# Loading the first K tile in four strided parts in a decode attention kernel

## Chip, cores, metric

One core of a Trainium2 chip. The metric is the device time of one execution in microseconds; lower is better. Executions of one kernel agree within 0.1% here (1271.40 to 1271.73 us for the kernel before), and all runs told below were in the fast state. Every set of runs was timed in rounds beside the kernel before on the same chip. In the names below PE is the tensor engine, DVE the vector engine, ACT the scalar engine, and SP the sync engine, which issues the large loads here.

## The reference, cut

A gated sum of one attention block at decode (one new token, a cache of 32,768 positions) and one small dense block.

```python
B, Sq, D = 2, 1, 448
Hq, Hkv, Sk, Dh = 16, 8, 32768, 256          # k_cache, v_cache: (B, Hkv, Sk, Dh), bf16
q = x @ wq                                   # (2, 16 heads, 256)
p = softmax(q k^T * Dh**-0.5);  a = (p v) @ wo
b = gelu(x @ w1 + b1) @ w2 + b2
out = g * a + (1 - g) * b                    # g = sigmoid((x * gate_w).sum(-1))
```

Each of the two caches is 268 MB; with the weights, the work is reading 547 MB once. Everything else is small.

## The kernel before: the parts that matter

K and V come in tiles of 16,384 positions. A tile has 128 partitions; partition p holds 128 consecutive positions of 256 values, that is one contiguous row of 65,536 bytes. Three slots of a ring in SBUF take the tiles in turn; SP issues all large loads.

```python
P, R = 128, 128
SLOT = R * Dh                                 # 32768 bf16 = 65,536 bytes per partition
ring = sb("ring", [P, NB * SLOT], dt.bfloat16)            # NB = 3

def kv_src(cache, idx):
    ...
    return cache[b, kvh, t*P*R:(t+1)*P*R, :].rearrange("(p r) d -> p (r d)", p=P)

def first_load(E):                            # placed ahead of the opening barrier
    s0 = slot_of[("K", 0)]
    E.ins(lambda e: e.dma_start(cut(s0, 0, SLOT), kv_src(A_k_cache, 0)),
          key=("fill", ("K", 0)), stream=f"slot{s0}")

def prog_sp(E):                               # then WQ, W1, K1, K2, V0, K3, V1, ...
    for d in order[1:]:
        for pd in before_of[d]:
            E.wait("pe", released(pd))        # until the slot is free
        ...
        dma(lambda e, ...: e.dma_start(cut(slot_of[d], 0, SLOT), src), f"slot{slot_of[d]}", ("fill", d))

def T(idx, blk):                              # DVE: first user of a K tile
    if blk == 0:
        wait_fill(E, ("K", idx))
    E.ins(lambda e: e.transpose(k_words(idx, blk), k_words(idx, blk)), key=("T", idx, blk))
```

The load queue (q1 in the profile) is one deep line, and its packets follow the order of issue: in the kernel before the first packet of WQ, 24,576 bytes long, starts at 21.01 us by the packet records, when all 128 rows of the first tile have started. SP puts the next tile in long before the last one has landed: K1 is issued at 2.78 us, and the last row of K0 ends at 21.8 us.

## Time and profile before

| | before |
|---|---|
| median (6 runs) | 1271.53 us |
| span of the profiled run | 1269.6 us |
| share of 16 DMA engines that the load queue fills | 99.8% |
| first K tile used | 22.17 us |
| time for one row of 65,536 bytes on one engine | 2.42 us |

The lines, and how they are read, are in the prediction.

### The profile page before, as it was taken

The numbers are of one execution on the slowest core, as the hardware profiler recorded it, in microseconds if no ns is written. First come the engines' busy times: TensorE is split into PE (matmuls) and PEld (weight loads), VectorE is DVE, ScalarE is ACT, GpSimd is POOL, SyncE is SP. The second block draws the span as 40 slices with busy tenths as digits, with TensorE's granted clock in tenths as the row PEclk, the third lists the DMA queues.
The fourth block names the chain that finished last, engine by engine and source line by source line (L and its number), as shares of the span: only waits on it lengthen the run. The fifth ranks groups of instructions, "written<-read, shape, count | busy, mean of one in ns | idle before, by whom it ended". The sixth has DMA issues, their size and how long they took to land.

```text
span 1269.6 us, 7458 instructions
## 1 busy us (share of the span) xinstructions
PE 699.4 (55%) x4386; PEld 141.0 (11%) x1842; DVE 690.0 (54%) x311; ACT 44.7 (4%) x184; POOL 4.4 (0%) x19
## 2 busy tenths in 40 slices
PE   0977457635466554665544665444664546655365
PEld 0211001100011110111000111000110001111012
DVE  4676536655365563556735467453755636557351
ACT  0100000000000000000000000000000000000000
POOL 1000000000000000000000000000000000000000
PEclk9888787776788677877767877778877678877787
DMA  9999999999999999999999999999999999999998
GB/s 407 451 429 428 432 432 432 447 432 428 429 432 434 438 432 440 434 432 429 432 429 442 432 436 438 432 429 429 432 442 432 434 440 432 429 429 432 442 424 371
DMA packets 11114, 547.58 MB, mean 431 GB/s; under 512 B 1368, under 2 KB 1632, under 8 KB 2144
## 3 DMA queue, kind: packets, MB, share of 16 engines
q1 hardware_dynamic: 10948, 547.43, 99.8%
q8 instruction: 7, 0.11, 0.0%
q10 hardware_dynamic: 156, 0.01, 0.0%
q14 instruction: 3, 0.02, 0.0%
HBM read 547.43 MB, written 0.00 MB: 431 GB/s over the span
## 4 chain that ended last, share of the span: by engine, by line
DMA 61%; PE 19%; DVE 14%; issue 5%; SPq 0%; ACT 0%; ACTq 0%
DMA ring<-in_A_k_cache_dram 57%; DVE ring L758 12%; PE ps_s L525 6%; PE ps_s L342 6%; PE ps_o L342 4%; DMA ring<-in_A_wo_dram 3%; DVE mx L762 1%; DMA PT<-in_gate_w_dram 1%; PE ps_o L574 1%; PE ps_m L539 0%; PE ps_m L534 0%; DVE gmax L764 0%; PE ps_o L468 0%; DVE gmx L768 0%; PE ps_o L439 0%
## 5 line engine op out<-in xcount | busy, mean ns | idle before, releaser
L758 DVE STREAM_TRANSPOSE ring<-ring 128x4096 uint32<-128x4096 uint32 x128 | 557.6, 4413 | 379.8 <-DMA ring<-in_A_k_cache_dram 379.6
L525 PE MATMUL ps_s<-ring,Abd 128*128 128x512 bf16 x1024 | 424.9, 415 | 399.9 <-DVE ring L758 399.4
L342 PE MATMUL ps_s<-ring,Abd 128*128 128x512 bf16 x1024 | 421.2, 411 | 0.0
L525 PEld LDWEIGHTS ps_s<-ring,Abd 128*128 128x128 bf16 x1024 | 105.7, 103 | 819.3 <-DVE ring L758 462.0
L342 PE MATMUL ps_o<-ring,PT 128*24 128x512 bf16 x1504 | 114.0, 411 | 0.0
L544 PE MATMUL ps_f<-o_sb,selg 128*32 128x257 f32 x32 | 17.0, 634 | 91.1 <-DVE o_sb L791 89.9
L574 PE MATMUL ps_o<-ring,PT 128*24 128x512 bf16 x544 | 57.9, 424 | 12.8 <-DMA ring<-in_A_v_cache_dram 12.8
L762 DVE TENSOR_REDUCE mx<-ps_s 128x1 f32<-128x1024 f32 x16 | 19.6, 1225 | 62.8 <-PE ps_s L342 62.8
L675 ACT ACTIVATE negm<-ps_m 128x1 f32<-128x1 f32 x16 | 2.7, 171 | 1131.8 <-PE ps_m L539 1131.8
L775 DVE STREAM_TRANSPOSE PT<-pexp 128x1024 bf16<-128x1024 bf16 x16 | 19.9, 1244 | 39.7 <-PE ps_o L342 39.7
L791 DVE TENSOR_REDUCE o_sb<-ps_o 128x256 f32<-128x2048 f32 x15 | 34.4, 2291 | 0.5
L789 DVE TENSOR_TENSOR ps_o<-ps_o,mask 128x2048 f32<-128x2048 f32 x15 | 34.3, 2290 | 0.0
L574 PEld LDWEIGHTS ps_o<-ring,PT 128*24 128x24 bf16 x544 | 14.7, 99 | 104.8 <-issue 87.9
L772 DVE COPY ls<-lsum 128x1 f32<-128x1 f32 x16 | 2.5, 154 | 32.1 <-ACT pexp L679 32.1
L669 ACT COPY Abd<-qrep 32x16 bf16 (+1 forms) x128 | 19.5, 199 | 0.6
L679 ACT ACTIVATE pexp<-ps_s,negm 128x1024 bf16<-128x1024 f32 x16 | 17.8, 1114 | 1.7
L534 PE MATMUL ps_m<-ident_f,mx 128*1 128x128 f32 x32 | 6.1, 271 | 21.1 <-DVE mx L762 21.1
L439 PE MATMUL ps_o<-ring,xT 128*32 128x512 bf16 x16 | 6.2, 608 | 20.5 <-issue 20.5
L544 PEld LDWEIGHTS ps_f<-o_sb,selg 128*32 128x32 f32 x32 | 2.9, 140 | 109.5 <-DVE o_sb L791 107.4
L539 PE MATMUL ps_m<-ones_f,gmx 1*128 1x1 f32 x32 | 6.4, 267 | 9.9 <-DVE gmx L768 9.9
L805 DVE TENSOR_SCALAR o_sb<-ps_o,mask 128x256 f32<-128x256 f32 x1 | 0.5, 484 | 15.6 <-PE ps_o L342 15.6
L764 DVE TENSOR_REDUCE gmax<-ps_m 1x2 f32<-1x128 f32 x16 | 4.4, 278 | 7.5 <-PE ps_m L534 7.5
(87 smaller groups left out, 78.0 us busy)
## 6 DMA issues: line engine op xcount, KB each, us to landing
ring<-in_A_v_cache_dram SPq DMA_DIRECT2D x1, 4096.0 KB, 27.2
ring<-in_A_v_cache_dram SPq DMA_DIRECT2D x2, 2048.0 KB, 34.0
ring<-in_A_wq_dram SPq DMA_DIRECT2D x1, 3072.0 KB, 28.6
ring<-in_B_w_dram SPq DMA_DIRECT2D x1, 1568.0 KB, 32.9
ring<-in_A_wo_dram SPq DMA_DIRECT2D x1, 1568.0 KB, 36.2
ring<-in_B_w_dram SPq DMA_DIRECT2D x1, 1344.0 KB, 32.2
ring<-in_A_wo_dram SPq DMA_DIRECT2D x1, 1008.0 KB, 38.2
ring<-in_A_wo_dram SPq DMA_DIRECT2D x1, 560.0 KB, 39.1
```

The source lines that it names most:

```text
L342: return e.add_instruction(mybir.InstMatmult(name=f"I-{nc.next_id()}", engine=mybir.EngineType.PE, ldweights=False, ins=[e.lower_ap(x), e. ...
L525: fn = lambda e, o=o, x=x, st=st, sp=sp, s=s, w=w: e.matmul(o, a_win(s, w), x, start=st, stop=sp, skip_group_check=True)
L539: E.ins(lambda e: e.matmul(ps_m[:, C_BC:C_BC + 1], gmx[:, :], ones_f[0:1, 0:1], start=True, stop=True), key=("M2", g))
L544: E.ins(lambda e: e.matmul(ps_oa, selg[:, :], o_sb[:, :], start=False, stop=False, skip_group_check=True), key=("OT", g))
L574: fn = lambda e, o=o, x=x, wt=wt, st=st, sp=sp, j=j: e.matmul(o, wt, x, start=st, stop=sp, skip_group_check=True)
L669: E.ins(lambda e, o=o, Q=Q, c=c: e.copy(o[:, :, c:c + 2], qrep[32 * Q:32 * Q + 32, :, bass.ds(E.dyn(2 * g, 2), 2)]), key=(("A", g) if (Q = ...
L679: E.ins(lambda e: e.activation(pexp[:, :].rearrange("p (r i a) -> p i r a", r=CR, i=2), ps_s[:, :].rearrange("p (i r a) -> p i r a", i=2, ...
L758: E.ins(lambda e: e.transpose(k_words(idx, blk), k_words(idx, blk)), key=("T", idx, blk))
L762: E.ins(lambda e: e.tensor_reduce(mx[:, :], ps_s[:, :], AX.X, ALU.max), key=("MX", g))
L775: E.ins(lambda e: e.transpose(PT[:, :], pexp[:, :]), key=("PT", g))
L789: E.ins(lambda e: e.tensor_tensor(p, p, mb, ALU.mult), key=("OM", g))
L791: E.ins(lambda e: e.tensor_reduce(o_sb[:, 0:Dh], ps_o[:, :].rearrange("p (n d) -> p d n", d=Dh), AX.X, ALU.add), key=("OS", g))
```

## The change

The intent, as far as the code tells it: let the first transfer be small, one row for each engine, then one more, two and four, so that the stream might start sooner. The partitions are taken in steps of 8, 8, 4 and 2: (0, 8, ..., 120), (4, 12, ..., 124), (2, 6, ..., 126), and all the odd ones.

```diff
         def first_load(E):
             s0 = slot_of[("K", 0)]
-            E.ins(lambda e: e.dma_start(cut(s0, 0, SLOT), kv_src(A_k_cache, 0)), key=("fill", ("K", 0)), stream=f"slot{s0}")
+            src = kv_src(A_k_cache, 0)
+            for i, (r, step) in enumerate(((0, 8), (4, 8), (2, 4), (1, 2))):
+                o = ring[r:P:step, s0 * SLOT:(s0 + 1) * SLOT]
+                E.ins(lambda e, o=o, r=r, step=step: e.dma_start(o, src[r:P:step, :]),
+                      key=(("fill", ("K", 0)) if i == 3 else f"fill{i}"), stream=f"slot{s0}")
```

## The prediction

The sum that was named had these terms: eight rows, each 2.42 us longer, +19.4 us; less 1 us that engines out of step were to give back; together +18.4 us and 1289.9 us; less a few tenths for an earlier start, 1289.5 us. That a row would take 2 x 2.42 us: take it, and what sets the rivals A, B and C apart, as assumption.

> **What bounds the kernel now**
>
> I read four views in this order: the page's rows by slice and by queue, the chain of work, the stretches of one microsecond at the start, and the order of time of the SP queue with what it waits for.
>
> The page first.
>
> ```profile
> span 1269.6 us, 7458 instructions
> ...
> DMA  9999999999999999999999999999999999999998
> GB/s 407 451 429 428 432 432 432 447 432 428 429 432 434 438 432 440 434 432 429 432 429 442 432 436 438 432 429 429 432 442 432 434 440 432 429 429 432 442 424 371
> ...
> q1 hardware_dynamic: 10948, 547.43, 99.8%
> ...
> DMA 61%; PE 19%; DVE 14%; issue 5%; SPq 0%; ACT 0%; ACTq 0%
> ```
>
> The queue of SP moves 547.43 MB and its packets fill 99.8% of what 16 engines have in the span. No slice falls below 9 tenths until the last one. PE (55%) and DVE (54%) are far from full. So the time is: the moment at which data begins to flow, plus 547.43 MB at the rate of the engines, plus the tail. Nothing that shortens compute can matter, and every microsecond that the DMA engines lose, wherever it is lost, comes out at the end, because there is no idle DMA time later in which to catch up.
>
> Then the first microseconds. Columns are PE, PEld, DVE, ACT, POOL busy, the clock, the DMA share and GB/s. A packet counts wholly in the stretch in which it starts.
>
> ```profile
> 0.00:1.00 1.00, 0.00 (x0) 0.00 (x0) 0.00 (x0) 0.00 (x0) 0.40 (x6) 1.00 0.00 0
> 1.00:2.00 1.00, 0.00 (x0) 0.00 (x0) 0.69 (x1) 0.00 (x0) 0.96 (x7) 1.00 3.17 1049
> 2.00:3.00 1.00, 0.00 (x0) 0.00 (x0) 1.00 (x1) 0.00 (x0) 1.00 (x3) 1.00 0.00 0
> 3.00:4.00 1.00, 0.00 (x0) 0.00 (x0) 1.00 (x8) 0.00 (x0) 1.00 (x5) 1.00 0.00 0
> 4.00:5.00 1.00, 0.00 (x0) 0.00 (x0) 0.26 (x1) 0.00 (x0) 0.85 (x4) 1.00 2.42 1049
> ```
>
> 1049 GB/s for 1 us is 1.049 MB, or 16 packets of 65,536 bytes: one row of K per engine (128 rows of 256 bf16). A share of 3.17 says that each of these first sixteen took 3.17 us; the second sixteen took 2.42 us each. So one row costs an engine 2.42 us (27.1 GB/s, times 16 is 433 GB/s, the rate of the whole run), and the first row about 0.75 us more, a start-up cost. All engines begin together and go in step: sixteen starts in one stretch, none in the next two, sixteen again.
>
> Last, the SP queue and the first use of the tile.
>
> ```profile
> 0.00 0.40 SPq L374 DMA_DIRECT2D ring<-in_A_k_cache_dram  x1
> 0.81 0.80 SPq L388 DMA_DIRECT2D ring<-in_A_wq_dram  x2
> 1.66 1.07 SPq L393 DMA_DIRECT2D ring<-in_B_w_dram  x2
> ...
> 22.17 17.42 DVE L758 STREAM_TRANSPOSE ring<-ring 128x4096 uint32<-128x4096 uint32 x4 [0.62 <-DMA ring<-in_A_k_cache_dram]
> ...
> SPq L100 <- PE ps_o L473: 42.5, 1, 42.5
> ...
> SPq L864 <- PEq L864: 0.8, 1, 0.8
> ```
>
> The first K tile is issued ahead of the opening barrier, in 0.40 us; the first packets start just after 1.0 us; the tile has landed by about 22.1 us. That is 1.05 + 3.17 + 7 x 2.42 = 21.2 us for the eight rows of an engine, and under 1 us to the semaphore and for late engines. SP then waits for PE at the barrier. The next load that waits for a buffer is issued at about 45.8 us.
>
> [...]
>
> **The change part by part**
>
> Removed: one issue of 0.40 us. Added: four. By the rows above an issue costs about 0.40 us (0.80 for two), so SP reaches the barrier at about 4 x 0.42 = 1.7 us in place of 0.4, and the barrier, which ended near 0.8 us, ends near 1.8 us. That delays the set-up on all engines by about 1 us. It costs nothing: the first tile is in the queue by then, DVE waits for it until 22 us, and the weights queue behind it.
>
> Start of the data: [...] The sixteen first packets all start between 1 and 2 us, so under 0.5 us can be gained.
>
> The bytes: the same 128 rows from the same addresses, the same 65,536-byte packets. If I divide each transfer in order, engine e gets row 8e, then 8e+4, then 8e+2 and 8e+6, then 8e+1, 8e+3, 8e+5 and 8e+7. [...]
>
> A row then takes an engine 2 x 2.42 = 4.84 us. For the tile: 8 x 2.42 = 19.4 us more. [...] Net +18.4 us. After the first tile everything is 128 partitions again and costs what it did. Because the DMA engines have no slack, the 18.4 us stand in the end: 1271.5 + 18.4 = 1289.9, and less a few tenths for the earlier start, 1289.5 us.
>
> The waits beside it: [...] the gate's weights, which landed at 19.25 us, would land near 38 us. The query weights, which follow the first tile, move from about 30.8 to about 50 us, so they still come later. The next load's wait (45.8 us) moves to about 65, while the queue then holds data until 54 + 19 = 73 us (8.4 MB, 3.7 MB, 1.6 MB and 8.4 MB at 433 GB/s end near 54 us now). So no second gap opens.
>
> **The rivals**
>
> A, no effect. The engines could be chosen by the partition itself[...]: the first two transfers then go to different engines and run at once, and all rows are moved as before. For it: the even 2.42 us of today. [...] Time 1271 to 1272 us; at best 0.5 us is gained from the start.
>
> B, half the effect. [...] Then only two rows cost double: 2 x 2.42 = +4.8 us, 1276 us. Or [...] anywhere from 1276 to 1288. [...]
>
> C, the main line: all eight rows at half rate, 1288 to 1291 us.
>
> D, worse than C: [...] the larger distance of 512 KB between the rows read at once (eight rows of 65,536 bytes) slows the reading as well. It would take 25.4 us to pass 2%, a factor of 2.3 on the tile. I see no line for it.
>
> **Range and chances**
>
> I give C 0.52, B 0.2, A 0.22, D 0.06. The time that I name is C's, 1289.5 us. The range from 1271.0 to 1292.5 covers A's lower edge up to a C without any relief (1271.5 + 19.4 = 1290.9), and nearly 9 in 10. It is wide because the distribution has two humps. Faster by 2% would need 25 us less than a stream that is already 99.8% full; that is excluded in practice, 0.005. Slower by over 2% is D, 0.055. Within 2%: 0.94.
>
> **What will show it right or wrong**
>
> In the stretches of 1 us: a second wave of packets that starts near 6.5 us, in place of 4-5 us, and shares near 4.8 in the first 40 us, show C. Double shares for two waves only show B; 3.17 and then 2.42 show A. The first transpose on DVE at about 41 us is C, 27 is B, 22 is A. The first two slices of the page's GB/s row should fall well below 400, the rest stay as they are. SP's first issue should be four, ended near 1.7 us, and the weights' issue begin near 1.9 us. The query's first matmul moves from 30.8 to about 50 us in C. I am wrong if [...] rows are not dealt out in order.

## The result, and the profile after

| | before | after |
|---|---|---|
| median (6 runs each) | 1271.53 us | 1276.65 us |
| lowest to highest | 1271.40 to 1271.73 | 1276.52 to 1277.01 |
| span of the profiled run | 1269.6 us | 1274.8 us |

The ratio is 1.0041 (95% interval 1.0028 to 1.0054). Ratios here are the mean time of one kernel's runs over that of the other's of the same rounds, so not quite the ratio of the medians. It is a loss of 5.1 us, well outside the noise and well within 2%. The direction and the verdict were as predicted; the size was not: 18.0 us were named.

The page of the changed kernel:

```profile
span 1274.8 us, 7471 instructions
...
GB/s 344 446 428 428 431 440 439 426 430 439 430 440 432 428 432 438 430 444 428 428 434 436 434 440 428 428 438 434 436 436 428 430 440 430 442 430 428 432 430 372
...
q1 hardware_dynamic: 10996, 547.43, 99.8%
```

The bytes are the same and the queue is still 99.8% "busy", though 5 us longer: a packet that takes twice as long counts as busy all that time (in the stretch from 5 to 10 us a share of 0.98 at 210 GB/s, where the kernel before has 0.97 at 420). Only the first slice fell, from 407 to 344 GB/s. A slice is 31.9 us, so 63 GB/s less are 2.0 MB, and 2.0 MB at 433 GB/s are 4.6 us. Nearly the whole loss lies in the first 32 us.

The stretches of 1 us at the start of the changed kernel (columns as in the prediction; the last two are DMA share and GB/s, each packet counted where it starts):

```profile
1.00:2.00 1.00, 0.00 (x0) 0.00 (x0) 0.00 (x0) 0.00 (x0) 0.00 (x0) 1.00 4.54 983
2.00:3.00 1.00, 0.00 (x0) 0.00 (x0) 0.00 (x0) 0.00 (x0) 0.00 (x0) 1.00 0.29 66
...
5.00:6.00 1.00, 0.00 (x0) 0.00 (x0) 1.00 (x8) 0.00 (x0) 1.00 (x3) 1.00 0.92 197
6.00:7.00 1.00, 0.00 (x0) 0.00 (x0) 0.20 (x2) 0.00 (x0) 0.91 (x4) 1.00 3.99 852
```

Fifteen packets start in the first stretch and one in the second. The share is that of 16 engines, so these sixteen take 4.54 + 0.29 = 4.83 us each on the mean. The next sixteen (3 + 13) take 0.92 + 3.99 = 4.9 us. In the kernel before these two numbers were 3.17 and 2.42. Sixteen rows that start together like this, one for each engine, are called a wave from here on. A transfer of 16 rows keeps all 16 engines busy (share 0.97 and 0.98 in the two stretches of 210 GB/s below), at half their speed: sixteen rows are in flight at a time, as before, and the queue holds 48 packets more (10,996 for 10,948), which are packets of 4 bytes, 16 for each of the three transfers more.

Then it stops. Stretches of 5 us, the first two of the kernel before and then four of the changed kernel:

```profile
0.00:5.00 5.00, 0.00 (x0) 0.00 (x0) 2.95 (x8) 0.00 (x0) 4.22 (x19) 1.00 1.12 419
5.00:10.00 5.00, 0.00 (x0) 0.00 (x0) 0.29 (x2) 0.00 (x0) 0.20 (x1) 1.00 0.97 420
```

```profile
0.00:5.00 5.00, 0.00 (x0) 0.00 (x0) 1.31 (x1) 0.00 (x0) 1.99 (x12) 1.00 0.97 210
5.00:10.00 5.00, 0.00 (x0) 0.00 (x0) 1.20 (x8) 0.00 (x0) 2.46 (x8) 1.00 0.98 210
10.00:15.00 5.00, 0.27 (x5) 0.21 (x5) 0.29 (x2) 1.45 (x2) 0.00 (x0) 1.00 1.07 420
15.00:20.00 5.00, 0.00 (x0) 0.00 (x0) 0.56 (x1) 0.00 (x0) 0.00 (x0) 1.00 0.98 420
```

210 GB/s for ten microseconds (one wave in each stretch), 420 from then on (two waves in each), as in the kernel before from the start. The first two transfers run at half rate; those of 32 and 64 rows at full rate. The order of time on SP and DVE of the changed kernel:

```profile
0.00 2.53 SPq L377 DMA_DIRECT2D ring<-in_A_k_cache_dram  x4
...
3.18 0.84 SPq L392 DMA_DIRECT2D ring<-in_A_wq_dram  x2
...
27.32 13.10 DVE L762 STREAM_TRANSPOSE ring<-ring 128x4096 uint32<-128x4096 uint32 x3 [5.61 <-DMA ring<-in_A_k_cache_dram]
```

The first transpose comes 5.15 us later (27.32 for 22.17), and the time is 5.12 us longer: what the first tile lost is what the kernel lost. The issues took 2.53 us in place of 0.40 and the barrier ended at about 3.2 us in place of 0.8. DVE still waited 5.61 us for the tile after its set-up was done, so the late barrier lies beside the transfer.

A ledger for one engine, as the mean of the sixteen packets of a wave, from the packet records of the two traces (us):

| | before | after | difference |
|---|---|---|---|
| first packet starts, from the span's start | 1.26 | 1.62 | +0.36 |
| row 1 | 3.17 | 4.83 | +1.66 |
| row 2 | 2.42 | 4.89 | +2.47 |
| row 3 | 2.42 | 2.86 | +0.44 |
| rows 4 to 8, each | 2.42 | 2.43 | +0.04 in all |
| gaps between them | | | +0.03 |
| row 8 ends | 21.37 | 26.38 | +5.0 |

### The profile page after: what moved, and what is told of

Same layout as the page of the kernel before. It is cut to its first block, busy times and chain, and to the rows that moved or that the text cites. A ratio compares the mean times of both kernels' runs of the same rounds, so it can differ in the third digit from the quotient of the medians.

```text
span 1274.8 us, 7471 instructions
## 1 busy us (share of the span) xinstructions
PE 702.1 (55%) x4386; PEld 141.2 (11%) x1842; DVE 689.6 (54%) x311; ACT 44.7 (4%) x184; POOL 4.4 (0%) x19
## 3 DMA queue, kind: packets, MB, share of 16 engines
q1 hardware_dynamic: 10996, 547.43, 99.8%
## 4 chain that ended last, share of the span: by engine, by line
DMA 61%; PE 17%; DVE 16%; issue 5%; another core or an unknown queue 0%; ACT 0%; SPq 0%; ACTq 0%
DMA ring<-in_A_k_cache_dram 57%; DVE ring L762 13%; PE ps_s L529 5%; PE ps_s L342 5%; PE ps_o L342 4%; DMA ring<-in_A_wo_dram 3%; DVE mx L766 1%; PE ps_o L578 1%; DMA PT<-in_gate_w_dram 1%; PE ps_m L543 0%; PE ps_m L538 0%; DVE gmax L768 0%; PE ps_o L472 0%; DVE gmx L772 0%
```

## The experiments

Theories. **Destination**: which partitions one transfer writes together decides its rate; a row takes twice as long in the two transfers of 16 partitions, 8 apart, and its usual time in those of 32 and 64. What in the hardware would make it so was assumed and is not shown. In the expectations the figures of this theory are those that come first. Rivals: **issues** (the three extra issues and the late barrier cost the time), **distance** (rows that are read at once lie 512 KB apart and disturb one another in the memory), **stride** (a step in the partitions slows engines by itself), and **start** (small transfers draw out the cold start of the stream). And, open from the prediction: whether the transfers of 32 and 64 lose anything when they are laid otherwise.

All edits are against the changed kernel. The loop is always the same; `a:z:step` are the partitions of the tile and the rows of the source.

### e1_w32: the two transfers of 16 become one of 32

```diff
-((0, 8), (4, 8), (2, 4), (1, 2))
+((0, 128, 4), (2, 128, 4), (1, 128, 2))       # a, z, step: 32, 32 and 64 rows
```

> The two transfers of 16 partitions become one of 32 with stride 4; the transfers of 32 and of 64 stay. [...] all eight waves of packets take about 2.42 us, the first about 3.2 us, and the time is within 0.7 us of the kernel before (1271 to 1272.3 us). Issue theory (the time comes from more issues ahead of the barrier, three extra cost 5.1 us): two extra cost about 3.4 us, 1275 us. Stride theory (any stride in the partitions slows the engines): slower by 5 us or more.

Measured: 1271.80 us (before, same rounds: 1271.52), ratio 1.0003 (0.9989 to 1.0017). From its stretches of 1 us and its order of time:

```profile
1.00:2.00 1.00, 0.00 (x0) 0.00 (x0) 0.00 (x0) 0.00 (x0) 0.00 (x0) 1.00 3.21 1049
```

```profile
0.00 1.83 SPq L379 DMA_DIRECT2D ring<-in_A_k_cache_dram  x3
...
22.47 17.42 DVE L764 STREAM_TRANSPOSE ring<-ring 128x4096 uint32<-128x4096 uint32 x4 [5.38 <-DMA ring<-in_A_k_cache_dram]
```

First wave 3.21 us, later ones 2.42 to 2.45 in the packet records, tile used at 22.47. The same rows in the same strides of 4 and 2, with 1.4 us more of issues than before: no loss. So neither these strides nor the issues cost anything (ratio 1.0003); the loss belongs to the two transfers of 16. The 0.3 us that are left are the later first packet (1.49 for 1.26 us) and some 0.08 us in the first two waves.

### e2_cols4: four transfers of the same bytes, cut by columns

```diff
+            lo = 0
+            for i, n in enumerate((16, 16, 32, 64)):
+                o = ring[:, s0 * SLOT + lo * Dh:s0 * SLOT + (lo + n) * Dh]
+                x = src[:, lo * Dh:(lo + n) * Dh]
+                lo += n
                 ...                                   # issued as in the change
```

> Four transfers with the same bytes each as in the change, but cut by columns: all 128 partitions with 16, 16, 32 and 64 of the 128 rows of 512 bytes. Same count of issues ahead of the barrier (about 2.4 us of SP time, barrier at about 3.2 us)[...]. [...] the tile lands as in the kernel before, first transpose at 22 to 23 us, time 1271 to 1272.5 us. Issue theory: all of it comes back, 1276 to 1277 us.

Measured: 1271.42 us, ratio 0.9999 (0.9985 to 1.0013).

```profile
0.00 1.88 SPq L380 DMA_DIRECT2D ring<-in_A_k_cache_dram  x4
...
21.92 17.42 DVE L765 STREAM_TRANSPOSE ring<-ring 128x4096 uint32<-128x4096 uint32 x4 [11.41 <-DMA ring<-in_A_k_cache_dram]
```

Four issues ahead of the barrier, which moves the weights' issue to 2.29 us, cost nothing. The issue theory is out. (An issue took 0.47 us on the mean here, from start to start, against 0.63 in the change, so the count is the same and the time of SP a little less.)

### e3_four16: four transfers of 16 in place of two

```diff
-((0, 8), (4, 8), (2, 4), (1, 2))
+((0, 128, 8), (4, 128, 8), (2, 128, 8), (6, 128, 8), (1, 128, 2))
```

> Four transfers of 16 with stride 8 (first partitions 0, 4, 2, 6), then one of 64 with stride 2: five issues. [...] four waves at 4.84 to 4.9 us in place of two, each 2.4 to 2.5 us over a normal one, so about +4.9 us on the change, that is +10 us on the kernel before, 1281 to 1282 us, first transpose at about 32 us. Issue theory: one more issue adds about 1.7 us, 1278.3 us.

Measured: 1281.88 us, +10.4 on the kernel before (ratio 1.0082). Stretches of 5 us:

```profile
10.00:15.00 5.00, 0.27 (x5) 0.21 (x5) 0.29 (x2) 1.45 (x2) 0.00 (x0) 1.00 1.00 210
15.00:20.00 5.00, 0.00 (x0) 0.00 (x0) 0.00 (x0) 0.00 (x0) 0.00 (x0) 1.00 1.00 210
20.00:25.00 5.00, 0.00 (x0) 0.00 (x0) 1.87 (x6) 0.20 (x1) 0.00 (x0) 1.00 1.07 420
```

Half rate for 20 us in place of 10. This run also splits the prediction in two: the rows 2, 6, 10, ... in one transfer of 32 ran at full rate; the same rows as two transfers of 16 run at half rate. How the rows are grouped into transfers decides, not which rows they are.

### e4_srcnear: the same destinations, source rows close together (wrong result)

```diff
+parts = ((0,128,8, 0,16,1), (4,128,8, 16,32,1), (2,128,4, 2,128,4), (1,128,2, 1,128,2))   # destination a,z,step; source a,z,step
```

> As the change, but the first two transfers read the rows 0 to 15 and 16 to 31 of the source, 64 KB apart, in place of every eighth row, 512 KB apart; the destinations stay. The result is wrong on purpose. [...] nothing changes, two waves of 4.8 to 4.9 us, 1276 to 1277 us. Distance theory (the rows read at once lie 512 KB apart and disturb one another in the memory): the waves fall back to about 3.2 and 2.42 us and the time to 1271 to 1272.5 us.

Measured: 1276.67 us, ratio 1.0040. In the packet records waves of 4.62 and 4.89 us, then 2.86 and 2.43; the first transpose at 27.31 us. Each is within 0.01 us of the changed kernel except the first wave, whose packets start 0.23 us later and take 0.21 us less. Its stretches of 5 us have the same rates:

```profile
0.00:5.00 5.00, 0.00 (x0) 0.00 (x0) 1.30 (x1) 0.00 (x0) 1.98 (x12) 1.00 0.92 210
5.00:10.00 5.00, 0.00 (x0) 0.00 (x0) 1.64 (x8) 0.00 (x0) 2.44 (x8) 1.00 0.98 210
10.00:15.00 5.00, 0.27 (x5) 0.21 (x5) 0.29 (x2) 1.45 (x2) 0.00 (x0) 1.00 1.07 420
```

Reading 64 KB apart changes nothing, so the distance in memory is not the cause; the destination is left. (The comparison with the reference still passed, although 31 partitions held other rows of K than they should: it does not tell such a mix-up from a right result here.)

### e5_halves and e6_comb: the same two sizes, neighbouring partitions or every second one

```diff
+((0, 64, 1), (64, 128, 1))      # e5_halves: neighbours
+((0, 128, 2), (1, 128, 2))      # e6_comb: every second one
```

> Two transfers of 64 neighbouring partitions, 0 to 63 and 64 to 127, so two issues. [...] all eight waves at about 4.85 us, 8 x 2.42 = 19.4 us more, first transpose at about 41 us, 1290 to 1291.5 us (the size that the prediction gave to the whole change). Rival ([...] the halves go to different engines and run at once): waves of 2.42 us and 1271 to 1272.5 us.

> Two transfers of 64 as well, but the even partitions and then the odd ones (stride 2): the same count, size and issues as the halves[...]. [...] all waves at 2.42 us after the first, 1271 to 1272.3 us. If two transfers of 64 or a stride cost something by themselves, it shows here.

Measured: halves 1292.76 us (ratio 1.0167), comb 1271.81 us (ratio 1.0002, 0.9989 to 1.0016). Stretches of 5 us of the halves, then of the comb:

```profile
15.00:20.00 5.00, 0.27 (x5) 0.22 (x5) 0.29 (x2) 1.28 (x1) 0.00 (x0) 1.00 1.02 210
20.00:25.00 5.00, 0.00 (x0) 0.00 (x0) 0.00 (x0) 0.17 (x2) 0.00 (x0) 1.00 1.01 210
```

```profile
15.00:20.00 5.00, 0.00 (x0) 0.00 (x0) 1.87 (x6) 0.20 (x1) 0.00 (x0) 1.00 0.97 420
```

This is the cleanest pair: same number of issues, same sizes, same bytes, 21 us apart. It also shows that the two halves do not run at once: they run one after the other, 16 packets in step, at 210 GB/s in each stretch of 5 us up to 40 us (share 0.97 to 1.03), and the tile is used at 43.59 us (22.44 for the comb). Which engine takes which row is in no record here.

The halves were 1.3 us over the top of the expectation: six of their eight waves took 5.11 to 5.12 us, not 4.85.

### e7_step1: the sizes of the change without strides

```diff
+((0, 16, 1), (16, 32, 1), (32, 64, 1), (64, 128, 1))
```

> The sizes of the change, 16, 16, 32 and 64, without the strides: partitions 0-15, 16-31, 32-63, 64-127. [...] two waves of about 4 x 2.42 = 9.7 us; [...] six waves of 4.85 us. 2 x 7.25 + 6 x 2.42 = 29 us more: about 1300.5 us, first transpose near 51 us, slower by 2.3%. Issue theory: as the change, 1276.6 us. [...]

Measured: 1300.82 us, ratio 1.0231 (1.0217 to 1.0245), slower by over 2%. The first wave in the stretches of 1 us:

```profile
1.00:2.00 1.00, 0.00 (x0) 0.00 (x0) 0.00 (x0) 0.00 (x0) 0.00 (x0) 1.00 8.59 1049
```

Sixteen packets of 8.59 us, then 9.29 in the packet records, then six waves of 5.0 to 5.7: after its start a row takes 9.3 us in a transfer to 16 neighbours and 5.0 to 5.7 us in those to 32 and 64 neighbours, where it takes 2.42 us in one to 32 partitions 4 apart or 64 partitions 2 apart (e1, e6). Same sizes as the change, so sizes and issues are not what counts. In the change the strides were not the fault: they halved the time of a wave of 16 rows compared with neighbouring partitions (4.89 for 9.29 us), and for 32 and 64 rows they removed the loss.

One control is missing: no run has a transfer to 16 partitions at full rate. That few rows in a transfer are not the cause by themselves rests on e5, where 64 rows run at half rate, and on this run, where 16 rows run at a quarter.

### e8_last16: the reverse order

```diff
+((1, 128, 2), (2, 128, 4), (0, 128, 8), (4, 128, 8))
```

> The four transfers of the change in the reverse order: 64, 32, 16, 16. [...] six waves at 2.42 us (the first about 3.2), then two at 4.85 to 4.9, the same +4.9 us with a spill of up to 0.5 us into the weights' packets behind them: 1276.2 to 1277 us. Start theory (the loss comes from the cold start of the stream, drawn out by small first transfers): the loss goes away, 1271.5 to 1272.5 us.

Measured: 1277.32 us, ratio 1.0047. Stretches of 5 us:

```profile
10.00:15.00 5.00, 0.27 (x5) 0.22 (x5) 0.29 (x2) 1.45 (x2) 0.00 (x0) 1.00 0.97 420
15.00:20.00 5.00, 0.00 (x0) 0.00 (x0) 1.65 (x5) 0.20 (x1) 0.00 (x0) 1.00 0.95 210
20.00:25.00 5.00, 0.00 (x0) 0.00 (x0) 0.22 (x1) 0.00 (x0) 0.00 (x0) 1.00 0.99 210
```

The half rate moves with the two transfers to the end of the tile. The start theory is out. It is 0.7 us above the change: the first wave, now of the transfer of 64, took 3.17 us again with its start-up surplus, and the weights' first packets behind the tile took 1.42 us in place of 0.91. Both were expected. That it is 0.3 us above the range is the later first packet (1.53 for 1.26 us), which the expectation left out.

### e9_eight16: every row of every engine in a transfer of 16

```diff
+tuple((r, 128, 8) for r in (0, 4, 2, 6, 1, 5, 3, 7))
```

> Eight transfers of 16 with stride 8, first partitions 0, 4, 2, 6, 1, 5, 3, 7: the order of rows that the prediction assumed for every engine. [...] all eight waves at 4.9 us, 8 x 2.45 = 19.6 us more, with a later first packet about +20, 1291 to 1292 us; together with the change (two such waves, +5.1) and the four (+10.4) a straight line of 2.5 us per wave. If more issues made up for it[...], less: 1284 to 1289 us.

Measured: 1291.87 us (before: 1271.59), +20.3, ratio 1.0160. Eight waves of 4.85 to 4.92 us. Two of the stretches of 5 us, all eight up to 40 us alike:

```profile
15.00:20.00 5.00, 0.27 (x5) 0.21 (x5) 0.29 (x2) 1.45 (x2) 0.00 (x0) 1.00 0.98 210
...
35.00:40.00 5.00, 0.00 (x0) 0.00 (x0) 0.00 (x0) 0.00 (x0) 0.00 (x0) 1.00 0.98 210
```

So with 0, 2, 4 and 8 waves at half rate (e1, the change, e3, e9) the kernel is 0.3, 5.1, 10.4 and 20.3 us slower: 2.5 us for each. This kernel does what the prediction assumed of the change, and its sum for that (1290.9 without relief) is within 1 us. Nothing came back in 40 us: the waves stayed at 4.86 to the last.

### e10_s4: sixteen partitions 4 apart in one half

```diff
+((0, 64, 4), (64, 128, 4), (2, 128, 4), (1, 128, 2))
```

> The change with its two transfers of 16 laid otherwise: stride 4 in partitions 0 to 60 and then in 64 to 124. [...] waves of 4.9 us and 1276.3 to 1277 us. [...] (waves of 64 neighbouring partitions took 5.11 us, those with stride 8 took 4.9): two waves of 5.1 us, 1277 to 1277.5 us.

Measured: 1276.50 us, ratio 1.0039; waves of 4.70 and 4.97 us, first transpose at 27.18 us. As the change (1276.65 us): sixteen partitions 4 apart in one half cost what sixteen 8 apart over the whole cost. The 5.11 us of the neighbouring halves is not explained by their lying in one half of the partitions and stays open.

### e11_cols2: a try for something better than both

```diff
+            for i, n in enumerate((16, 112)):      # columns, all 128 partitions; the rest as in e2
```

> Two transfers of all partitions, cut by columns: 16 of the 128 rows of 512 bytes, then 112. A try for a kernel that beats both: the cut into four by columns had its first transpose 0.25 us earlier than the kernel before. [...] no loss, 1271.2 to 1271.7 us; nothing over 0.3 us can be gained, since only the first packets' surplus of 0.75 us is at stake.

Measured: 1271.29 us (before: 1271.59), ratio 0.9998 (0.9985 to 1.0012); the first transpose at 21.79 us against 22.17. The tile lands 0.4 us earlier, but the runs of the two kernels overlap (1271.21 to 1271.55, and 1271.41 to 1271.73) and the interval holds 1: nothing is shown in the time. If the intent of the change is worth anything, these runs leave room for no more than this.

## Why the prediction was right or wrong

**The bound** was right. The stream of loads sets the end, and every microsecond that the first tile lost appeared in the time: +5.15 at the first transpose, +5.12 at the end.

**The size of the slowdown** was right where there was one: 4.83 and 4.89 us for a row in the change where 2 x 2.42 = 4.84 was named, and 4.85 to 4.92 us for all eight in e9. That the partitions of the destination decide it is shown by e1 and e3 to e10; what in the hardware makes it so is not shown.

**The step that failed** is in "The change part by part": "If I divide each transfer in order", and the conclusion from it, that all eight rows are slowed. That holds for the two transfers of 16. It does not hold for those of 32 and 64: in e1 and e6 every row after the first took 2.42 to 2.45 us, and in e3 the transfer of 64 after its first row 2.42 to 2.43. The term "8 x 2.42 = 19.4 us" should have been two rows. Measured: +1.66 and +2.47 for the two, and +0.44 for the third row. Where the 0.44 come from is not shown; a like surplus follows the last half-rate wave in e3 (2.88 us) and e4 (2.86 us), and the weights' packets behind it in e8 (1.42 for 0.91 us).

The prediction had this as its rival B, at 1276 us with chance 0.2, and preferred in-order dealing without a line of the trace for it: the trace only held transfers of 128 rows. Neither B nor C had more than assumption behind it. The interval then had its upper part in the wrong place, but did contain the result.

That rival B's +4.8 us comes so near to the measured +5.1 is in part luck. The two rows cost 4.13 us, since the first has no start-up surplus on top; the later start (0.36 us), the third row (0.44) and small rests make up the difference.

**Terms that were off in size but did not decide**: the relief of 1 us is not seen; in e9 all eight rows took 4.85 to 4.92 us, none less than 4.84. The earlier start turned into a later one: the first packet starts at 1.62 us, not 1.26. An issue took 0.59 us, not 0.40, so SP reached the barrier at 2.53 us, not 1.7. The stride alone is not the reason: in e5, without one, the issues took 0.57 and 0.58 us and the first packet started at 1.50. In the runs whose first issue took 0.40 us (before, e2, e7, e11) the first packet starts at 1.17 to 1.26, in all others (0.56 to 0.64 us) at 1.48 to 1.85; what makes an issue longer stays open. The late barrier was rightly held to cost nothing, as e2 shows. The start-up surplus of the first row (0.75 us) did not add to the doubled row: 4.83 us is all of it. Why is open.

**The waits beside it**: no gap opened, as predicted. SP's wait for its next buffer ended near 51 us, well before the queue ran dry (near 54 + 5 = 59 us by the prediction's sum). The query's first matmul moved by 5 us, from 30.82 to 35.80, as the tile did. The gate's weights were named for 38 us and hardly moved: DVE used them at 19.44 us, for 19.28 before. Even in e9, which does what the prediction assumed for every row, they were used at 27.32 us. So this term was wrong by itself, and why is not shown. It cost nothing: in the changed kernel what DVE makes of them was done at 21.7 us, before the tile landed.

## What to carry to other kernels

When a load is cut up, cut it by columns and leave every part all partitions (e2: 1271.42 us, ratio 0.9999). If it has to be cut by partitions, time each part: here 64 partitions 2 apart and 32 partitions 4 apart took 2.42 us a row, 16 partitions 8 apart 4.9 us, 64 neighbours 5.1 us and 16 neighbours 9.3 us. A DMA queue at 99.8% says nothing of its speed (it did so at 2.42 and at 4.89 us a row): compare the time of one packet of known size with the same packet elsewhere in the trace. When the trace does not show how the rows of a transfer are treated, price both ways and don't let the longer chain of reasoning win.
